# Late constants, filler products and another place for one maximum in a three-stage kernel of attention, mixture of experts and MLP

## The chip, the cores and the metric

The kernel runs on one core of a Trainium2 chip. The time is that of one execution on the device, in microseconds (us). Its engines are TensorE (PE), VectorE (DVE), ScalarE (ACT), GpSimd (POOL) and SyncE (SP, which here only issues transfers). Each runs its own instructions in the order in which they are written, and waits for the others by semaphores.

## The reference

Three stages in a row: an attention over 32 memory slots, a mixture of 8 experts of which each token takes its two best, and a dense MLP.

```python
# attention: q, k, v (4, 8, 576, 64), phi (4, 8, 576, 32)
a = exp(phi - max(phi, axis=seq));  a /= sum(a, axis=seq) + 1e-9
k_m = einsum('bhsm,bhsd->bhmd', a, k);  v_m = einsum('bhsm,bhsd->bhmd', a, v)
attn = softmax(q @ k_m.T / 8);  x = (attn @ v_m)  as (2304, 512)
# experts: w1 (8, 512, 1024), w2 (8, 1024, 512)
logits = x @ w_gate + log1p(exp(x @ w_noise)) * noise
top2, weights = the two largest of 8, softmax over the two
x = sum over the two of weight * (relu(x @ w1[e]) @ w2[e])
# MLP: w_in (512, 2048), w_out (2048, 512)
h = x @ w_in;  out = (h * clip(h + 3, 0, 6) / 6) @ w_out
```

## The kernel before

Attention runs in 8 groups, each one batch and 4 of its heads. A group has the stages a1 (phi transposed and its exponential, L541), q (q transposed on PE, L557), a2 (the weights e transposed on DVE, L579, then the product km of k and v with them on PE, 144 small matmuls, L585, and kd from it, L589), b (scores and softmax, with POOL's multiplications at L634 and L643) and c (output, written to DRAM as xf, L650 to L677). A routing (L686) follows two batches each: logits, the two largest, and each token's place in its expert's list, by one-hot products on PE (L737 to L799) with the constants tri, io12 and tok12. It ends in lists of token numbers, ids0 for the first two tiles of expert 0 after the first two batches, and ids for all.

An expert takes up to 608 tokens, 5 tiles. Its rows are gathered by an indirect DMA that POOL issues (L840), transposed on PE (L857) for experts 0 and 1 and by DMA for the others. Layer 1 (L874) and layer 2 (L924) split each 32-bit value into two 16-bit ones; for layer 1 each PSUM result is evacuated twice by ACT (L881 hf, L882 hh) and once by DVE (L884). Two tiles of expert 0 run early, beside the second routing. A weight matrix (w1 or w2 of an expert) comes in four pieces of 1 MB; its absolute maximum gives a power-of-two scale (`scale_w`, L424), and ACT (L418) and DVE (L420) write its two halves. The maximum over partitions goes either over PE (a diagonal of the 128 maxima, wdg, times ones, L434, and a reduction on DVE) or over POOL (an all-reduce, L438).

The order of work is made ahead of time by a list scheduler in the kernel's own code (`Sched`, L92). Operations are listed in program order with estimated durations and dependences; `sch.op(engine, duration, function, reads, writes)` lists one. The number `rush` of an operation shifts its due time, and `ORDER` (L37) says at which step which stage of which group is listed. What is not listed, as all constants here (L306 to L350), stands ahead of everything else on its engine. Among the constants are 34 warm-up products of 128 columns on PE (L303), DVE's ident, identh, identb, tri, p6, tok and ioc, POOL's casts io12 and tok12, and an all-reduce `first` whose result isn't used.

Of the kernel before, what the change touches and what calls it, by code (L numbers as in the profile page):

```python
# [35 lines left out]
CG = 2.0 ** -25  # L36
ORDER = (('ld', -1), ('b', 1), ('r', 6), ('q', 0), ('a1', -1), ('c', 3), ('a2', 0))  # L37
W0 = (4, 9)
# [5 lines left out]
WARM = 34  # L44
RUSH = {'w0': -15.0, 'w1': -346.0, 'r0': 121.0, 'r1': 173.0, 'x0': 103.0, 'e1': -46.0, 'e2': 203.0, 'a': (-50.0, -60.0, -45.0, -20.0, -30.0, -25.0, 40.0, -30.0)}
W0G = (4, 7)
CDMA = 1
EAT = (9, 12, 13)

# [216 lines left out]
def dve(n, mode=1):  # L266
    return 0.15 + n / 960.0 / mode
# [15 lines left out]
def attn_moe_kernel(ctx, tc, q, k, v, phi, w_gate, w_noise, noise, w1, w2, w_in, w_out, out):  # L283
# [16 lines left out]
    with tc.tile_pool(name="warm", bufs=1, space=bass.MemoryType.PSUM) as wp:  # L300
        pw = wp.tile([128, 128], F32, name="pw")
        for i in range(WARM):
            PE.matmul(pw, onesh, onesh, start=True, stop=True)  # L303

# [13 lines left out]
    identh = const.tile([128, 128], F16, name="identh")  # L318
    DVE.tensor_copy(identh, ident)
    identb = const.tile([128, 128], BF16, name="identb")  # L320
    DVE.tensor_copy(identb, ident)
    onesb = const.tile([128, 128], BF16, name="onesb")
# [10 lines left out]
    tri = const.tile([PT, PT], F16, name="tri")  # L333
    DVE.tensor_scalar(tri, iof[:PT, :PT], iop[:PT, 0:1], None, op0=ALU.is_gt)
    tok = const.tile([PT, B * NJ], F32, name="tok")
    p6 = const.tile([PT, 1], F32, name="p6")
    DVE.tensor_scalar(p6, iop[:PT, 0:1], float(NJ), float(-NT // 2), op0=ALU.mult, op1=ALU.add)
    for b in range(B):
        DVE.tensor_scalar(tok[:, b * NJ:(b + 1) * NJ], iof[:PT, :NJ], p6, float(S * b), op0=ALU.add, op1=ALU.add)
    ef = iof[:PT, :NE]  # L340
    ioc = const.tile([PT, NE * NTI], F32, name="ioc")
    DVE.tensor_scalar(ioc, iof[:PT, :NE * NTI], float(BIG * NTI), None, op0=ALU.subtract)
    io12 = const.tile([PT, 128 + NE * NTI, 2 * NJ], F16, name="io12")
    POOL.tensor_copy(io12[:, :128], iof[:PT, :, None].to_broadcast([PT, 128, 2 * NJ]))
    POOL.tensor_copy(io12[:, 128:], ioc[:, :, None].to_broadcast([PT, NE * NTI, 2 * NJ]))
    tok12 = const.tile([PT, B // 2, 2 * NJ], F16, name="tok12")
    POOL.tensor_copy(tok12, tok.rearrange("p (b j) -> p b j", b=B // 2))

    first = const.tile([128, 1], F32, name="first")
    POOL.partition_all_reduce(first, c3, channels=128, reduce_op=RED.absmax)  # L350
    bsum = const.tile([PT, B // 2, NE], F16, name="bsum")
# [37 lines left out]
    def new(nm, shape, dtype=F32):  # L389
        return T[nm].new(shape, dtype)  # L390
# [33 lines left out]
    def scale_w(am, deps, inv=2.0 ** -13, pe=False):  # L424
# [4 lines left out]
        if sch.seg == 0 or pe:  # L429

            wd, px = new("wdg", [128, 128], BF16), new(PS[sch.seg][2], [128, 128])
            sch.op("DVE", 0.25, lambda: DVE.tensor_scalar(wd.t, identb, ar.t[:, 0], None, op0=ALU.mult), [(ar, 0)], [wd],
                   lat=2.0 if inv < 1.0 else 0.0)
            sch.op("PE", 0.06, lambda: PE.matmul(px.t, onesb, wd.t, start=True, stop=True), [wd], [px], lat=0.12)  # L434
            sch.op("DVE", dve(128), lambda: DVE.tensor_reduce(ar.t[:, 1], px.t, axis=AX.X, op=ALU.max), [px], [(ar, 1)])  # L435
            pow2_ops(lambda: sm.t, lambda: DVE.tensor_scalar(sm.t[:, 0], ar.t[:, 1], TINY, None, op0=ALU.max), sm, [(ar, 1)], inv)
            return sm
# [28 lines left out]
    def stage_w1(e, w=None, acts=()):  # L466
        return stage_w(w1[e].rearrange("(c p) f -> p c f", p=128), "st0", w, acts)

# [72 lines left out]
    def stage_a1(g, ld):  # L541
# [144 lines left out]
    def route(b):  # L686
# [48 lines left out]
        def f():  # L735
# [4 lines left out]
            for j in range(NR - 1):  # L740
                n = NR - 1 - j
                PE.matmul(pv[:, j + 1:], onesh[:PT, :PT], mh.t[:, j, None, :].to_broadcast([PT, n, NE]),
                          start=False, stop=(n == 1))
        sch.op("PE", 1.0, f, [mh] + sums[:b] + [padk] * b, [pc])

# [38 lines left out]
        for h in range(2):  # L784
            ohb = new("ohb", [PT, 128 + 2 * nn, n12], F16)
            pv = lambda k, h=h: pqh.t[:, k, h][:, None, :]
            dv(64 * n12, lambda ohb=ohb, pv=pv: DVE.tensor_tensor(
                ohb.t[:, :128], io12[:, :128], pv(0).to_broadcast([PT, 128, n12]), op=ALU.is_equal), [(pqh, 0)], [(ohb, 0)])
            dv(nn // 2 * n12, lambda ohb=ohb, pv=pv: DVE.tensor_tensor(
                ohb.t[:, 128:128 + nn], io12[:, 128:], pv(1).to_broadcast([PT, nn, n12]), op=ALU.is_equal),  # L790
                [(pqh, 1)], [(ohb, 1)])
            dv(nn // 2 * n12, lambda ohb=ohb: DVE.tensor_tensor(
                ohb.t[:, 128 + nn:], ohb.t[:, 128:128 + nn],
                tok12[:, b][:, None, :].to_broadcast([PT, nn, n12]), op=ALU.mult),
                [(ohb, 1)], [(ohb, 2)])

# [40 lines left out]
    def gather(e, t0, nt, xT, idx, ikey, xfdeps, rows=NT):  # L837
        for t in range(nt):
# [6 lines left out]
            if e >= TDMA:  # L845
# [480 lines left out]
```

## Time and profile before

| | us |
|---|---|
| median of 3 runs | 914.17 (913.0 to 914.32) |
| profiled execution | 912.39 |
| its span, first to last instruction | 910.2 |
| PE busy | 874.0 |
| DVE busy | 617.8 |
| ACT busy | 436.8 |
| POOL busy | 142.6 |

The trace is of the profiled execution. Where a row of the timeline has several instructions of one line in a row, they are one row with their count; its duration reaches from the start of the first to the end of the last. A bracket at a row's end says how long the engine idled ahead of it, and what released it. PEclk is the clock granted to PE, 1.00 for 2.4 GHz and 0.50 for 1.2 GHz.

### The profile page before, as it was taken

Reading aid. Unit: us, or ns where it says so; the run is one execution under the profiler, and the core shown is the slowest. Engines: PE = TensorE matmul, PEld = TensorE weight load, DVE = VectorE, ACT = ScalarE, POOL = GpSimd, SP = SyncE. Lnnn points to the kernel's source line nnn. Section 1 sums busy time; section 2 is a strip of 40 time slices with the busy share of each in tenths; the row PEclk is TensorE's granted clock in tenths of the full one; section 3 lists DMA queues with packets and bytes.
Section 4 is the critical chain, followed back from the end, with each engine's and each line's share of the span. In section 5 each row is a group of like instructions: output and inputs, shape, how many; then the busy total and the mean of one; then the engine's idle time right before and its main releaser. Section 6 shows DMA issues by size and latency. Waiting matters only on the chain. (4 is left out here: it accounts for less than half of the span.)

```text
span 910.2 us, 16317 instructions
## 1 busy us (share of the span) xinstructions
PE 874.0 (96%) x6612; PEld 516.3 (57%) x6612; DVE 617.8 (68%) x1088; ACT 436.8 (48%) x665; POOL 142.6 (16%) x156
## 2 busy tenths in 40 slices
PE   7899599989999999999999999999999999999997
PEld 6676375564746565565756555555555555555553
DVE  5798975959688868688798889886464543333332
ACT  2386426656756657383646555554332422322322
POOL 2234311312032211000001131442010000000000
PEclk8999799999999999999999999999999999999999
DMA  9955335858878676949567463462210300300101
GB/s 343 351 187 175 101 122 202 270 147 254 224 201 274 157 262 169 274 93 295 196 244 221 159 221 133 114 150 59 75 38 1 79 1 10 61 1 1 35 1 38
DMA packets 109537, 135.14 MB, mean 148 GB/s; under 512 B 53008, under 2 KB 74000, under 8 KB 109456
## 3 DMA queue, kind: packets, MB, share of 16 engines
q1 hardware_dynamic: 103200, 114.43, 40.9%
q0 software_dynamic: 6144, 19.40, 7.7%
q8 instruction: 54, 0.88, 0.4%
q14 instruction: 27, 0.22, 0.1%
q10 hardware_dynamic: 112, 0.20, 0.1%
HBM read 94.74 MB, written 27.86 MB: 135 GB/s over the span
## 5 line engine op out<-in xcount | busy, mean ns | idle before, releaser
L1015 PE MATMUL two<-xT,wa 128*128 128x384 f16 x1152 | 195.1, 326 | 0.0
L1041 PE MATMUL o<-wb,hh 128*128 128x512 f16 x864 | 194.1, 379 | 0.0
L1015 PEld LDWEIGHTS <-wa 128*128 128x128 f16 x1152 | 112.6, 98 | 79.5 <-DVE hh L1025 0.2
L1041 PEld LDWEIGHTS <-hh 128*128 128x128 f16 x864 | 84.1, 98 | 96.3
L924 PEld LDWEIGHTS <-hh 128*128 128x128 f16 x720 | 69.7, 98 | 80.2 <-issue 2.5
L1022 ACT ACTIVATE hf<-hf,c 128x768 f32<-128x768 f32 x48 | 44.9, 935 | 145.2 <-DVE hf L1020 135.0
L1020 DVE TENSOR_TENSOR hf<-two,ivb 128x768 f32<-128x768 f32 x48 | 45.9, 956 | 92.1 <-PE two L1015 92.1
L874 PE MATMUL two<-xT,wb 128*128 128x304 f16 (+2 forms) x768 | 103.8, 295 | 3.3 <-ACT hh L882 3.2
L874 PEld LDWEIGHTS <-wb 128*128 128x128 f16 x768 | 75.8, 99 | 31.5 <-issue 3.9
L874 PEld LDWEIGHTS <-wa 128*128 128x128 f16 x768 | 75.9, 99 | 29.7 <-DVE war L435 1.7
L874 PE MATMUL two<-xT,wa 128*128 128x304 f16 (+1 forms) x672 | 90.1, 295 | 0.5 <-DVE war L435 0.5
L924 PE MATMUL o<-wb,hh 128*128 128x512 f16 x384 | 86.3, 379 | 0.0
L884 DVE TENSOR_TENSOR hh<-hf,hh 128x608 f16<-128x608 f32 (+2 forms) x72 | 49.5, 689 | 45.6 <-ACT hh L882 38.2
L924 PE MATMUL o<-wa,hh 128*128 128x512 f16 x336 | 75.3, 379 | 0.0
L840 POOL DMA_INDIRECT xg<-xf,ids x40 | 51.5, 1288 | 142.9 <-DVE ya L849 71.7
L881 ACT ACTIVATE hf<-two 128x608 f32<-128x608 f32 (+2 forms) x72 | 42.9, 596 | 55.3 <-PE two L874 53.0
L1025 DVE SCALAR_TENSOR_TENSOR hh<-hf,two 128x768 f32<-128x768 f32 x48 | 45.7, 951 | 29.8 <-ACT hf L1022 29.7
L1028 DVE TENSOR_TENSOR hh<-hh,hh 128x768 f16<-128x768 f32 x48 | 45.9, 955 | 29.4 <-ACT hh L1027 29.4
L1027 ACT ACTIVATE hh<-hh 128x768 f16<-128x768 f32 x48 | 40.4, 842 | 40.3 <-DVE hh L1025 40.3
L420 DVE SCALAR_TENSOR_TENSOR wb<-st,wsm,wb 128x1024 f16<-128x1024 f32 x40 | 50.5, 1280 | 4.5 <-ACT wb L418 3.2
L420 DVE SCALAR_TENSOR_TENSOR wa<-st,wsm,wa 128x1024 f16<-128x1024 f32 x40 | 51.3, 1310 | 1.4 <-ACT wa L418 1.4
L418 ACT ACTIVATE wb<-st,wsm 128x1024 f16<-128x1024 f32 x40 | 44.6, 1143 | 8.8 <-DVE wsm L406 3.6
(221 smaller groups left out, 1075.8 us busy)
## 6 DMA issues: line engine op xcount, KB each, us to landing
st<-moe_w_d SPq DMA_DIRECT2D x32, 1024.0 KB
ys<-yt SPq DMA_DIRECT2D x32, 256.0 KB
w<-moe_w_in_d SPq DMA_DIRECT2D x16, 512.0 KB
wf<-w64o SPq DMA_DIRECT2D x32, 256.0 KB
w<-moe_w_out_d SPq DMA_DIRECT2D x16, 512.0 KB
st<-wf SPq DMA_DIRECT2D x8, 1024.0 KB
kv<-k_d SPq DMA_DIRECT2D x8, 576.0 KB
kv<-v_d SPq DMA_DIRECT2D x8, 576.0 KB
```

The lines of the kernel that those rows point to most:

```text
L418: sch.op("ACT", act(1024, ptr=1), lambda s=s, w=w, c=c: ACT.activation(w.t[:, 0, c], s.t[:, c], AF.Copy, scale=sm.t[:, 2]), [(s, i), (sm, ...
L420: sch.op("DVE", 1.28, lambda s=s, w=w, c=c: DVE.scalar_tensor_tensor(w.t[:, 1, c], s.t[:, c], sm.t[:, 2], w.t[:, 0, c], op0=ALU.mult, op1= ...
L840: sch.op("POOL", 1.05, lambda t=t, xg=xg, tw=tw: POOL.indirect_dma_start(out=xg.t[:tw], out_offset=None, in_=xf[:rows], in_offset=bass.Ind ...
L874: PE.matmul(ph.t[:, i, :nw], wa.t[:, wi, c * 1024 + fb * 128:c * 1024 + fb * 128 + 128], xT.t[:, 4 * xi + c, o0 + i * nw:o0 + (i + 1) * nw ...
L884: sch.op("DVE", dve(n), lambda: DVE.tensor_tensor(hh.t[:, 1], hf.t, hh.t[:, 0], op=ALU.subtract), [hf, (hh, 0)], [(hh, 1)])
L924: PE.matmul(py.t[:tw], hs[fb].t[:, hi, tsl], wb.t[:, wi, fb * 512:(fb + 1) * 512], start=(fb == 0 and n == 0), stop=(fb == 7 and n == 2))
L1015: PE.matmul(ph.t[:, i, :CW], win[fb // 8].t[:, wi, o:o + 128], xT.t[:, 4 * xi + kc, :CW], start=(n == 0), stop=(n == 11))
L1020: sch.op("DVE", dve(768), lambda: DVE.tensor_tensor(t1.t, ph.t[:, :, :CW], ivb.t[:, None, :CW].to_broadcast([128, 2, CW]), op=ALU.mult), [ ...
L1022: o = sch.op("ACT", act(768, ptr=1), lambda: ACT.activation(t1.t, t1.t, AF.Relu, bias=c3, scale=CG), [], [t1])
L1025: sch.op("DVE", dve(768), lambda: DVE.scalar_tensor_tensor(gf.t, t1.t, 6.0 * CG, ph.t[:, :, :CW], op0=ALU.min, op1=ALU.mult), [t1, ph], [gf])
L1028: sch.op("DVE", dve(768), lambda: DVE.tensor_tensor(g.t[:, 1], gf.t, g.t[:, 0], op=ALU.subtract), [gf, (g, 0)], [(g, 1)])
L1041: PE.matmul(po[m_].t, g.t[:, gi, i, m_ * 128:(m_ + 1) * 128], wou[fb // 8].t[:, wi, (fb % 8) * 512:(fb % 8 + 1) * 512], start=(fb == 0 and ...
```

## The change

The warm-up gets ten more products of 512 columns. Before the first early transposes PE gets three listed operations of five products of 512 columns each, of ones with ones, into the transposes' own PSUM tile; they depend on ids0. Six constants become listed operations, DVE's four behind the transposed weights e of group 0, POOL's two behind DVE's. `first` is dropped. The maximum of the third expert's w1 (`e == 2`) goes over PE instead of POOL. The tables that set the listing change as a whole; of them the routing's step in ORDER (6 to 5) and the early layer's in EAT (12 to 11) stand for the others.

```diff
-ORDER = (('ld', -1), ('b', 1), ('r', 6), ('q', 0), ('a1', -1), ('c', 3), ('a2', 0))
+ORDER = (('b', 1), ('q', 0), ('c', 3), ('a2', 0), ('ld', -1), ('a1', -1), ('r', 5))
 WARM = 34
+WARM2 = 10
+FILL = 3
-EAT = (9, 12, 13)
+EAT = (9, 11, 13)
...
-        pw = wp.tile([128, 128], F32, name="pw")
+        pw = wp.tile([128, 4, 128], F32, name="pw")
         for i in range(WARM):
-            PE.matmul(pw, onesh, onesh, start=True, stop=True)
+            PE.matmul(pw[:, 0], onesh, onesh, start=True, stop=True)
+        for i in range(WARM2):
+            PE.matmul(pw, onesh, onesh[:, None, :].to_broadcast([128, 4, 128]), start=True, stop=True)
...
-    first = const.tile([128, 1], F32, name="first")
-    POOL.partition_all_reduce(first, c3, channels=128, reduce_op=RED.absmax)
...
-        return stage_w(w1[e].rearrange("(c p) f -> p c f", p=128), "st0", w, acts)
+        return stage_w(w1[e].rearrange("(c p) f -> p c f", p=128), "st0", w, acts, e == 2)
...
+    def late_consts(after):
...
+        for eng, dur, fn, r, w in (
+                ("DVE", 0.45, idb, [], idbk),
+                ("DVE", 0.3, lambda: DVE.tensor_scalar(tri, iof[:PT, :PT], iop[:PT, 0:1], None, op0=ALU.is_gt), [], trik),
+                ("DVE", 0.22, lambda: DVE.tensor_scalar(ioc, iof[:PT, :NE * NTI], float(BIG * NTI), None, op0=ALU.subtract),
+                 [], iock),
+                ("DVE", 0.75, toks, [], tokk),
+                ("POOL", 2.2, io, [iock], io12k),
+                ("POOL", 0.2, lambda: POOL.tensor_copy(tok12, tok.rearrange("p (b j) -> p b j", b=B // 2)), [tokk], tok12k)):
+            o = sch.op(eng, dur, fn, r, [w])
+            if eng == "DVE":
+                o.after.add(after)
...
-        sch.op("DVE", dve(576), lambda: DVE.transpose(e.t.rearrange("p i m -> p (i m)"), aT.t), [aT], [e])
+        o = sch.op("DVE", dve(576), lambda: DVE.transpose(e.t.rearrange("p i m -> p (i m)"), aT.t), [aT], [e])
+        if g == 0:
+            late_consts(o)
...
             px = new(PS[sch.seg][2], [128, 4, 128])
+            if sch.seg == 0 and e == 0 and t0 + t == 0:
+
+                for _ in range(FILL):
+                    def f(px=px):
+                        for _ in range(5):
+                            PE.matmul(px.t, onesh, onesh[:, None, :].to_broadcast([128, 4, 128]), start=True, stop=True)
+                    sch.op("PE", 1.07, f, [ikey], [px])
```

How the order moves is seen at three places. On DVE at the start, first before, then with the change (st holds a group's sums, aT its exponentials, e their transpose; L545 is L536 after, L579 is L598, L553 is L544):

```order
L317 TENSOR_SCALAR ident<-iof,iop 128x128
L334 TENSOR_SCALAR tri<-iof,iop 96x96
L319 CAST identh<-ident 128x128
L321 CAST identb<-ident 128x128
L337 TENSOR_SCALAR p_151<-iop 96x1
L339 TENSOR_SCALAR tok<-iof,p_151 96x6 x4
L545 STREAM_TRANSPOSE aT_209<-ph_196 128x576
L546 TENSOR_REDUCE st_214<-aT_209 128x1
L579 STREAM_TRANSPOSE e_224<-aT_209 128x576
L552 TENSOR_SCALAR st_214<-st_214 128x1
L553 RECIPROCAL st_214<-st_214 128x1
```

```order
L321 TENSOR_SCALAR ident<-iof,iop 128x128
L536 STREAM_TRANSPOSE aT_205<-ph_192 128x576
L537 TENSOR_REDUCE st_210<-aT_205 128x1
L598 STREAM_TRANSPOSE e_220<-aT_205 128x576
L543 TENSOR_SCALAR st_210<-st_210 128x1
L544 RECIPROCAL st_210<-st_210 128x1
L558 CAST identb<-ident 128x128
L559 CAST identh<-ident 128x128
L566 TENSOR_SCALAR tri<-iof,iop 96x96
L567 TENSOR_SCALAR ioc<-iof 96x40
L536 STREAM_TRANSPOSE aT_304<-ph_197 128x576
```

The five constants that stood ahead of group 0's transpose now stand behind its reciprocal, around group 1's transpose; ioc comes later too.

On ACT in layer 1 of the second expert (L881 and L882 evacuate a result, L847 prepares gathered rows of the third expert, L418 is the first scaled copy of a piece of the third expert's w1, wa), before and after (there L909, L910, L868 and L409):

```order
L881 ACTIVATE hf_2593<-two_2521 128x608
L882 ACTIVATE hh_2595<-two_2521 128x608
L418 ACTIVATE wa_2597<-st_3_2362,wsm_2563 128x1024
L847 ACTIVATE ya_2600<-xg_2513 128x512
L881 ACTIVATE hf_2627<-two_2566 128x608
L882 ACTIVATE hh_2630<-two_2566 128x608
L418 ACTIVATE wa_2597<-st_3_2362,wsm_2563 128x1024
```

```order
L909 ACTIVATE hf_2760<-two_2700 128x608
L910 ACTIVATE hh_2765<-two_2700 128x608
L868 ACTIVATE ya_2768<-xg_2616 128x512
L909 ACTIVATE hf_2778<-two_2735 128x608
L910 ACTIVATE hh_2780<-two_2735 128x608
L496 ACTIVATE w64a_2794<-w_2_2621 128x512
L868 ACTIVATE ya_2874<-xg_2690 128x512
L409 ACTIVATE wa_2879<-st_3_2385,wsm_2872 128x1024 x4
```

The four copies of w1 stood between the evacuations and now stand behind the last of the layer.

On POOL at the first all-reduce of a weight's maximum (war; an ISA row without a tile is the configuration instruction ahead of it, L840 or L861 a gather), before and after:

```order
L840 DMA xg_2432<-xf,ids 128x512
L840 DMA xg_2513<-xf,ids 128x512
L840 DMA xg_2546<-xf,ids 96x512
L438 ISA
L438 ISA war_2550<-war_2550 128x1
L840 DMA xg_2558<-xf,ids 128x512
L840 DMA xg_2632<-xf,ids 128x512
```

```order
L861 DMA xg_2690<-xf,ids 128x512
L861 DMA xg_2762<-xf,ids 128x512
L861 DMA xg_2782<-xf,ids 128x512
L861 DMA xg_2882<-xf,ids 96x512
L429 ISA
L429 ISA war_2935<-war_2935 128x1
L429 ISA war_3069<-war_3069 128x1
```

The configuration and the first all-reduce move behind the five gathers of the next expert, and the all-reduce is now that of the third expert's w2.

## Rows read from the trace of the kernel before

**Rows 1.** The page, busy time of each engine.
```profile
PE 874.0 (96%) x6612; PEld 516.3 (57%) x6612; DVE 617.8 (68%) x1088; ACT 436.8 (48%) x665; POOL 142.6 (16%) x156
```

**Rows 2.** Windows: busy us of PE, PEld, DVE, ACT, POOL; PEclk, DMA share, GB/s.
```profile
8.00:9.00 1.00, 0.00 (x0) 0.00 (x0) 0.33 (x1) 0.63 (x2) 0.00 (x0) 0.70 1.01 406
9.00:15.00 6.00, 5.45 (x104) 5.49 (x108) 2.39 (x7) 0.87 (x2) 0.00 (x0) 0.50 1.06 359
46.00:91.00 45.00, 42.69 (x785) 31.78 (x783) 41.26 (x110) 34.68 (x65) 16.40 (x14) 1.00 0.54 179
104.00:117.00 13.00, 6.13 (x29) 4.07 (x28) 10.47 (x33) 6.21 (x9) 3.35 (x2) 0.50 0.23 58
193.00:196.00 3.00, 3.00 (x14) 1.77 (x13) 3.00 (x4) 3.00 (x5) 0.32 (x1) 0.50 0.72 175
229.00:400.00 171.00, 171.00 (x1250) 106.18 (x1248) 130.26 (x199) 104.85 (x158) 29.54 (x26) 1.00 0.72 208
```

**Rows 3.** Timeline of PE: start us, us, what, and idle time before.
```profile
0.99 3.81 PE L303 MATMUL pw<-onesh 128*128 128x128 f16 x34 [0.99 <-POOL onesh L299]
...
9.55 6.88 PE L585 MATMUL oa<-kv,e 32*32 32x128 f32 x144 [4.74 <-DVE st L552]
...
37.40 4.13 PE L585 MATMUL oa<-kv,e 32*32 32x128 f32 x144
```

**Rows 4.** Timeline of DVE and POOL at the start.
```profile
3.29 1.50 POOL L344 CAST io<-iof 96x1536 f16<-96x1536 f32 x1
3.30 1.56 DVE L334 TENSOR_SCALAR tri<-iof,iop 96x96 f16<-96x96 f32 x1
...
6.18 0.77 DVE L545 STREAM_TRANSPOSE aT<-ph 128x576 f32<-128x576 f32 x1
...
22.49 1.16 POOL L634 TENSOR_TENSOR sc<-sc,sm 128x576 f32<-128x576 f32 x1 [15.73 <-DVE sm L633]
```

**Rows 5.** DMA from 0 to 30 us: GB/s in 40 slices of 0.75 us.
```profile
GB/s 0 0 101 316 412 381 332 338 338 390 384 406 418 436 374 208 301 316 393 424 409 406 399 412 439 363 388 349 396 436 409 406 350 140 31 74 326 406 406 326
```

**Rows 6.** Timeline of PE, POOL and DVE at the first gather and early layer.
```profile
105.06 1.35 POOL L840 DMA_INDIRECT xg<-xf,ids  x1 [7.64 <-DMA xf<-hl]
...
108.79 1.09 PE L857 MATMUL oa<-ident,xg 128*128 128x128 f32 x4 [4.51 <-DMA xg<-xf,ids]
111.19 1.09 PE L857 MATMUL oa<-ident,xg 128*128 128x128 f32 x4 [1.31 <-DMA xg<-xf,ids]
...
113.69 5.89 PE L874 MATMUL da<-xT,wa 128*128 128x256 f16 x35 [0.36 <-DVE xT L861]
...
117.40 0.23 DVE L727 TENSOR_TENSOR mh<-mk 96x96 f16<-96x96 f32 x1
...
119.41 0.21 PE L737 MATMUL oa<-mh,tri 96*96 96x96 f16 x1
...
120.16 4.09 PE L874 MATMUL da<-xT,wa 128*128 128x256 f16 x36
...
132.50 5.34 PE L924 MATMUL oa<-wa,hhe 128*128 128x512 f16 x24
```

**Rows 7.** L438's instructions, then the timeline of POOL, PE and ACT around it.
```profile
L438 POOLq MODIFY_POOL_CONFIG  x2: 43/43/43, 182.3 to 182.3; - x2
...
182.78 6.62 PE L874 MATMUL two<-xT,wb 128*128 128x304 f16 x50
188.72 0.41 POOL L438 PARTITION_ALL_REDUCE war<-war  x1 [6.70 <-issue]
189.72 1.15 ACT L418 ACTIVATE wa<-st,wsm 128x1024 f16<-128x1024 f32 x1 [5.23 <-DVE wsm L406]
192.57 7.64 PE L874 MATMUL two<-xT,wb 128*128 128x304 f16 x45 [3.16 <-ACT hh L882]
203.53 2.75 PE L924 MATMUL o<-wb,hh 128*128 128x512 f16 x12
...
227.06 3.26 PE L874 MATMUL two<-xT,wa 128*128 128x304 f16 x24
```

More of the change, by code (lines that the diff above doesn't have):

```diff
@@ L44 @@
 WARM = 34
-RUSH = {'w0': -15.0, 'w1': -346.0, 'r0': 121.0, 'r1': 173.0, 'x0': 103.0, 'e1': -46.0, 'e2': 203.0, 'a': (-50.0, -60.0, -45.0, -20.0, -30.0, -25.0, 40.0, -30.0)}
+WARM2 = 10
+FILL = 3
+RUSH = {'w0': -22.0, 'w1': -195.0, 'r0': 256.0, 'r1': 623.0, 'x0': 357.0, 'e1': -60.0, 'e2': 195.0, 'a': (-35.0, -40.0, -45.0, -25.0, -20.0, -10.0, 110.0, -5.0)}
 W0G = (4, 7)
 CDMA = 1
-EAT = (9, 12, 13)
+EAT = (9, 11, 13)
 def _atanh_coefs(n=5):
@@ L318, in attn_moe_kernel @@
     identh = const.tile([128, 128], F16, name="identh")
-    DVE.tensor_copy(identh, ident)
     identb = const.tile([128, 128], BF16, name="identb")
-    DVE.tensor_copy(identb, ident)
     onesb = const.tile([128, 128], BF16, name="onesb")
@@ L333, in attn_moe_kernel @@
     tri = const.tile([PT, PT], F16, name="tri")
-    DVE.tensor_scalar(tri, iof[:PT, :PT], iop[:PT, 0:1], None, op0=ALU.is_gt)
     tok = const.tile([PT, B * NJ], F32, name="tok")
     p6 = const.tile([PT, 1], F32, name="p6")
-    DVE.tensor_scalar(p6, iop[:PT, 0:1], float(NJ), float(-NT // 2), op0=ALU.mult, op1=ALU.add)
-    for b in range(B):
-        DVE.tensor_scalar(tok[:, b * NJ:(b + 1) * NJ], iof[:PT, :NJ], p6, float(S * b), op0=ALU.add, op1=ALU.add)
     ef = iof[:PT, :NE]
     ioc = const.tile([PT, NE * NTI], F32, name="ioc")
-    DVE.tensor_scalar(ioc, iof[:PT, :NE * NTI], float(BIG * NTI), None, op0=ALU.subtract)
     io12 = const.tile([PT, 128 + NE * NTI, 2 * NJ], F16, name="io12")
-    POOL.tensor_copy(io12[:, :128], iof[:PT, :, None].to_broadcast([PT, 128, 2 * NJ]))
-    POOL.tensor_copy(io12[:, 128:], ioc[:, :, None].to_broadcast([PT, NE * NTI, 2 * NJ]))
     tok12 = const.tile([PT, B // 2, 2 * NJ], F16, name="tok12")
-    POOL.tensor_copy(tok12, tok.rearrange("p (b j) -> p b j", b=B // 2))
-    first = const.tile([128, 1], F32, name="first")
-    POOL.partition_all_reduce(first, c3, channels=128, reduce_op=RED.absmax)
     bsum = const.tile([PT, B // 2, NE], F16, name="bsum")
@@ L431, in scale_w @@
             wd, px = new("wdg", [128, 128], BF16), new(PS[sch.seg][2], [128, 128])
-            sch.op("DVE", 0.25, lambda: DVE.tensor_scalar(wd.t, identb, ar.t[:, 0], None, op0=ALU.mult), [(ar, 0)], [wd],
+            sch.op("DVE", 0.25, lambda: DVE.tensor_scalar(wd.t, identb, ar.t[:, 0], None, op0=ALU.mult), [(ar, 0), idbk], [wd],
                    lat=2.0 if inv < 1.0 else 0.0)
@@ L555, in stage_a1, with toks, idb, io @@
         return st, aT
+    idbk, trik, tokk, iock, io12k, tok12k = [sch.keep() for _ in range(6)]
+    def late_consts(after):
+        def toks():
+            DVE.tensor_scalar(p6, iop[:PT, 0:1], float(NJ), float(-NT // 2), op0=ALU.mult, op1=ALU.add)
+            for b in range(B):
+                DVE.tensor_scalar(tok[:, b * NJ:(b + 1) * NJ], iof[:PT, :NJ], p6, float(S * b), op0=ALU.add, op1=ALU.add)
+        def idb():
+            DVE.tensor_copy(identb, ident)
+            DVE.tensor_copy(identh, ident)
+        def io():
+            POOL.tensor_copy(io12[:, :128], iof[:PT, :, None].to_broadcast([PT, 128, 2 * NJ]))
+            POOL.tensor_copy(io12[:, 128:], ioc[:, :, None].to_broadcast([PT, NE * NTI, 2 * NJ]))
+        for eng, dur, fn, r, w in (
[9 more added lines that the diff above has]
+                o.after.add(after)
     def stage_q(g, ld):
@@ L743, in f @@
                           start=False, stop=(n == 1))
-        sch.op("PE", 1.0, f, [mh] + sums[:b] + [padk] * b, [pc])
+        sch.op("PE", 1.0, f, [mh, trik] + sums[:b] + [padk] * b, [pc])
         def count(terms, keys, fn, w):
@@ L787, in route @@
             dv(64 * n12, lambda ohb=ohb, pv=pv: DVE.tensor_tensor(
-                ohb.t[:, :128], io12[:, :128], pv(0).to_broadcast([PT, 128, n12]), op=ALU.is_equal), [(pqh, 0)], [(ohb, 0)])
+                ohb.t[:, :128], io12[:, :128], pv(0).to_broadcast([PT, 128, n12]), op=ALU.is_equal), [(pqh, 0), io12k], [(ohb, 0)])
             dv(nn // 2 * n12, lambda ohb=ohb, pv=pv: DVE.tensor_tensor(
                 ohb.t[:, 128:128 + nn], io12[:, 128:], pv(1).to_broadcast([PT, nn, n12]), op=ALU.is_equal),
-                [(pqh, 1)], [(ohb, 1)])
+                [(pqh, 1), io12k], [(ohb, 1)])
             dv(nn // 2 * n12, lambda ohb=ohb: DVE.tensor_tensor(
@@ L794, in route @@
                 tok12[:, b][:, None, :].to_broadcast([PT, nn, n12]), op=ALU.mult),
-                [(ohb, 1)], [(ohb, 2)])
+                [(ohb, 1), tok12k], [(ohb, 2)])
             def f(ohb=ohb, h=h):
```

## The prediction

> **What bounds the kernel now.** I read the page first: TensorE (PE) is busy for 874.0 of 910.2 us [rows 1], so what a change of order can win lies in the 36 us in which PE stands, and in the stretches in which it runs at half its clock. The table of windows says where these are: from 229 us on PE has no gap (171.00 of 171.00 us in 229 to 400), while the granted clock is 0.50, the lower of its two levels (1.2 instead of 2.4 GHz), in 9 to 15, 104 to 117 and 193 to 196 us [rows 2]. Each of these three follows a standstill of PE, and the timeline of each place says what PE waited for.
>
> At the start, 34 warm products end at 4.80 (0.99 + 3.81). PE then idles 4.74 us to 9.55, when the first km product (L585) has its operand. The product takes 6.88 us; the same 144 matmuls take 4.13 later [rows 3]. At the first gather, PE waits 4.51 and 1.31 us for gathered rows, and the first 35 products of the early layer run at 5.89 us where 36 later take 4.09 [rows 6]. At the third expert's first weight, PE waits 3.16 us and runs slowly after it [rows 7]. Between the first two, from 46 to 91 us, VectorE (DVE) and PE share the limit, busy 41.26 and 42.69 of the 45 us [rows 2]; work that enters this stretch earlier leaves it earlier if neither gets more to do.
>
> **The start.** Before, DVE runs tri, identh, identb, p6 and tok ahead of group 0's first transpose (L545), which starts at 6.18; from there to the product at 9.55 is a chain of 3.37 us [rows 3, 4]. The change puts these constants behind group 0's transposed weights. DVE is then free at about 3.3, where tri starts, and the chain alone would give a product at 6.7. It also needs phi, k and v of group 0, together 1.47 MB (288, 576 and 576 KB). The transfer rates of 0.75 us each sum to 1.41 MB by 6.0 us and 2.15 MB by 8.0 [rows 5]. Served strictly in order the operands are there at 6.2; if the transfers share the engines with the ones issued behind them (phi of group 1, then q, 2.36 MB with these) v comes later. I take 8.0, between 6.7 and the 9.55 of before, since what lies ahead of v and half of what follows is through by then: gain 1.5 us, bounds 0 and 2.85.
>
> The warm block grows by ten products of 512 columns. At 24 in 5.34 us [rows 6] they take 2.2 us, so PE works to 7.0 and idles some 1.0 us instead of 4.74. Before, the clock held for the first 3.2 us of idling: it is mixed, 0.70, only in the slice 8 to 9 [rows 2]. I expect it to hold, and km to take 4.13 instead of 6.88: gain 2.75, bounds 0 and 2.75. Sum of the start: 4.25 us.
>
> Is this handed on? The constants (2.9 us of DVE before, from 3.30 to 6.18, standing beside POOL among it) fall where DVE waits: it ran 2.39 us in the six from 9 to 15 [rows 2]. The transfers up to v of group 1 are 3.5 MB, which the rates reach before 12 us [rows 5], ahead of a second product at 15.3 (19.6 less 4.25). So the cover holds; if it fails, all 4.25 are lost, which is the first rival.
>
> Two prices hang on the move. First, GpSimd's (POOL's) casts into io12 now run beside group 1's DVE work. In the trace tri, 96x96, took 1.56 us beside the first cast of 1.50 [rows 4], though DVE's operations of this size on the routing take 0.23, as mh [rows 6]. POOL's casts are this one, 1,536 columns, and one of 480, some 2.0 us at that rate. So up to 2.0 us of DVE can be blocked near 8 to 10.5 us, and group 1's next need is at km's end, 12.1; DVE would then be late by 0 to 0.7 us. I take 0. The Trainium skill, SBUF — State Buffer, "SBUF: two separate sides", says why this can recur: VectorE in some modes and GpSimd share a port pair as an exclusive lock, and whoever comes second stands for the whole instruction. The trace's 1.56 beside 1.50 agrees, and by the rule the sum would be 0.7 us smaller. Second, the configuration instruction ahead of POOL's first tensor_tensor has its cost hidden somewhere in the 15.73 us that POOL waits for DVE until 22.49 [rows 4]. It now stands behind the casts, at about 10.6. At the 6.4 us that the other configuration of the trace took (182.3 to 188.72, [rows 7]) it is over at 17.0, before the need at 18.2 (22.49 less 4.25), 7.6 after 10.6. Cost 0, with an upper end of 15.7 - 7.6 = 8.1 us.
>
> **Routing, fillers and the first gather.** The first gather starts at 105.06; its last releaser by the trace is the write of xf, not ids0 [rows 6]. Listing route(0) a step sooner moves about six of its DVE operations, of mh's 0.23 us each, ahead of attention work, some 1.4 us, but if xf's write binds, the gather comes no sooner. I take 0, bounds 0 and -1.4 us. The fillers are 15 products of 512 columns behind ids0 and ahead of the first transposes: 3.3 us at full clock, 6.7 at half. They need ids0 alone, which the gather needs too, so they start no later than it, and the rows arrive 3.7 us after 105.06 (at 108.79): at full clock nothing is delayed. At half clock the first transposes come 3.0 us late, but the second, at 111.19, wait for their own rows; the end slips by 0.5 at most. What they buy is the clock. 35 products at full clock take 35/36 of 4.09 = 3.98, so 1.91 us is won there, and half of the second transposes' 1.09, together 2.4. Next in the way is the routing of the last batches: its mh ended at 117.63 and its product L737 ran at 119.41 [rows 6], so 1.8 us of slack is met by products 2.4 us earlier, and up to 0.6 is given back, since mh's chain itself waits for evacuations of these products only in part. Gain 1.8, bounds +0.5 (a loss) and -3.8 us with the earlier list.
>
> **The third expert.** Before, w1's maximum is an all-reduce on POOL, which idles 6.70 us after its configuration at 182.3 and starts at 188.72. DVE's L440 stands for it, and the first scaled copy on ScalarE (ACT, L418) behind that for 5.23 us to 189.72. Behind this copy in ACT's order are the evacuations of expert 1's layer 1, so PE stops for 3.16 us [rows 7]. Then 45 products take 7.64 us; at the 6.62/50 of those before it is 5.96, so the clock costs 1.68. The change takes this maximum with a PE product of 128 columns (0.2 us) in layer 2, and its four ACT copies stand behind all eight pairs of evacuations. Gain 3.16 + 1.68 = 4.84 us, bounds 3.2 and 4.84: the clock's part depends on the standstill alone.
>
> The configuration isn't saved, it moves to w2 of the third expert. There it stands behind 20 gathers, in layer 2 of expert 1, by the order some 6 us after that layer's start. At 6.4 us it ends at about 12.8, the scale is out at 15 to 16, and four copies of 1.15 us on ACT end at 20. Behind them in ACT's order are outputs of later tiles and then expert 2's first evacuation, which was due 23.5 us after layer 2's start (203.53 to 227.06, [rows 7]). So some 3 us of cover are left, and I count 0. The Trainium skill, GPSIMD Engine Reference, "2.1 Instruction dispatch", says that the first call into freshly loaded GpSimd code pays about 6 us of loading that no instruction shows. The trace agrees (6.4 us to the start, 6.70 idle). By that rule each change of POOL's code pays again wherever it stands, and with the cover gone the third expert's gain would be 0.
>
> **Sum.** 4.25 + 1.8 + 4.84 = 10.9 us. The profiled run took 912.39 (its span 910.2 and 2.2 around it), the median is 914.17, so the one gives 901.5 and the other 903.3. I predict at the median: **903.3 us**. Least gains: 0 + 0 (with -0.5) + 3.2, less 0.7, is 2.0; most: 5.6 + 3.8 + 4.84 = 14.2.
>
> **Rivals.**
> - The start's gain is lost, all or in part (chance 0.20). The warm block ends before v arrives by more than I think, and the clock falls anyway: 906.1. Or group 1 waits for its own transfers and all 4.25 goes: 907.6. For it: the DMA engines are full from 2 to 24 us. Against: the sums of [rows 5].
> - POOL's configuration takes back in layer 2 what it gave in layer 1 (0.10). If the loading starts 3 us later than I read it, ACT's copies reach expert 2's evacuations; at 6 to 7 us later PE stops again for 3.2 and runs slow for 1.7: 908.1. For it: the cover is the thinnest of all. Against: the gathers ahead of it are listed for an expert two steps on.
> - Slower than before (0.07): POOL's configuration ahead of group 0's first tensor_tensor really takes the 15.7 us that the trace leaves room for. Then attention stands 8.1 us at the start, the clock falls again, the half-clock prices come back (2.75 for a km product and 1.7 for what follows), and POOL's casts add their 0.7: 914.2 - 10.9 + 8.1 + 4.5 + 0.7 = 916.6, with no change ending at 916.0. It decides from a load of some 15 us; under 7.6 it costs nothing. The single load that the trace shows took 6.4.
> - The change doesn't do what it says (0.07): the numbers of the planner also move weight preparation of the later experts. PE has no gap there today, so they can only cost; 9 to 11 us of new waits would end at 912 to 914, of which 0.05 is within the bound.
>
> **How the numbers follow.** The forecast has 0.56. The lower end is 900.0: 903.3 less 1.4 for the sooner gather and 1.3 for the start's bound, and 0.6 for mh, is 900.0. The upper end is 909.0, which takes in the first two rivals with the 0.7 of the casts. About 0.18 is left out. A difference of 0.2%, 1.8 us, is about what can be told from no change. Faster than 912.3: 0.56 + 0.20 + 0.10 + 0.02 = 0.88; same 0.05; slower 0.07.
>
> **What will show it.** Right: the first km product starts near 8 us and takes 4.1; the granted clock is 1.00 in 9 to 15; the first early products run at 0.114 us each; no wait of PE for ACT in expert 1's layer 1, and the all-reduce's 6.7 us standing in layer 2 with PE at work. Wrong: a km product of over 6 us, a DVE or POOL wait of several us at 17 to 25 us, a first gather that isn't 4 us sooner than 105.06, or new PE waits beyond 229 us.

## The result and the profile after

The changed kernel takes 904.02 us at the median (902.5 to 905.97), the kernel before in the same comparison 913.95; the ratio is 0.9905 with a 95% interval from 0.9888 to 0.9921. Forecast was 903.3 us, a gain of 10.9; measured is 9.9. Two later comparisons gave 0.9897 (0.9873 to 0.9922) and 0.9898 (0.9880 to 0.9916), gains of 8.5 and 8.9 us. The sum came out nearly right. Its terms did not: each of the three was forecast too large.

The profiled execution of the changed kernel took 905.97 us with a span of 904.2. The page of after, busy time of each engine (before: [rows 1]):

```profile
span 904.2 us, 16357 instructions
PE 878.0 (97%) x6638; PEld 516.9 (57%) x6638; DVE 617.7 (68%) x1090; ACT 436.4 (48%) x665; POOL 144.5 (16%) x154
```

PE idles 26 us instead of 36. Its timeline at the start (before: [rows 3]):

```profile
0.99 3.81 PE L305 MATMUL pw<-onesh 128*128 128x128 f16 x34 [0.99 <-POOL onesh L301]
4.59 2.92 PE L307 MATMUL pw<-onesh 128*128 128x512 f16 x10
8.17 4.13 PE L606 MATMUL oa<-kv,e 32*32 32x128 f32 x144 [0.66 <-DMA kv<-v_d]
...
15.44 3.89 PE L606 MATMUL oa<-kv,e 32*32 32x128 f32 x130
21.20 0.63 PE L606 MATMUL oa<-kv,e 32*32 32x128 f32 x14 [1.87 <-issue]
...
26.34 5.74 PE L606 MATMUL oa<-kv,e 32*32 32x128 f32 x144
```

The first km product starts at 8.17 and takes 4.13 us, as forecast. But the third takes 5.74: the half clock has come back, later. The windows of after in five stretches (columns as in [rows 2]; the clock is the third number from the end) show where:

```profile
6.00:15.00 9.00, 7.44 (x179) 5.75 (x176) 5.28 (x20) 2.39 (x6) 0.78 (x2) 1.00 1.04 360
20.00:30.00 10.00, 7.10 (x122) 5.42 (x126) 6.86 (x22) 3.65 (x8) 2.31 (x2) 0.83 1.03 393
87.00:97.00 10.00, 6.96 (x37) 4.62 (x36) 9.51 (x42) 3.66 (x8) 5.00 (x7) 0.83 0.44 123
100.00:118.00 18.00, 13.53 (x91) 8.92 (x92) 15.27 (x49) 8.10 (x17) 4.54 (x5) 0.81 0.47 154
190.00:198.00 8.00, 7.40 (x56) 5.28 (x54) 6.98 (x10) 4.95 (x10) 2.81 (x2) 1.00 1.10 315
```

To see where the time went I cut the span of two profiles of before (this one and run r5) and three of after (this one, r1 and r9) at the starts of the same PE instructions: the first routing's second group of one-hot products, the second routing's product with tri (L737 before, L758 after), expert 0's layer 1 on its late tiles, expert 2's layer 1. Us from one to the next, gains by the means:

| stretch | before | after | gain | forecast |
|---|---|---|---|---|
| start to one-hot products | 103.18, 102.89 | 101.48, 100.68, 99.61 | 2.45 | 4.25 |
| to second routing's product | 16.23, 16.02 | 15.53, 15.26, 15.61 | 0.66 | 1.8 |
| to expert 0's layer 1 | 23.02, 23.00 | 23.00, 23.00, 23.00 | 0.0 | 0 |
| to expert 2's layer 1 | 84.63, 84.23 | 80.80, 80.54, 80.49 | 3.82 | 4.84 |
| to the end | 683.14, 684.06 | 683.39, 683.32, 683.49 | 0.2 | 0 |

That is 7.1 us; the medians say 8.5 to 9.9, 9.1 in the mean. The profiled executions of after lie 0 to 2 us above the medians of their runs (905.97 to 904.02, 904.55 to 904.55, 904.02 to 902.95), 1.0 in the mean; those of before lie 0.6 below theirs in the mean (912.39 to 913.95, 912.29 to 911.95); and the time outside the span is 0.4 us shorter after (1.8 instead of 2.1 to 2.2). Together these are the difference. What the new listing of the tables contributes to each stretch was not tried apart from the named changes.

### The profile page after: what moved, and what is told of

It is laid out like the page before. It is cut to its first block, busy times and chain, and to the rows that moved or that the text cites. A ratio compares the mean times of both kernels' runs of the same rounds, so it can differ in the third digit from the quotient of the medians.

```text
span 904.2 us, 16357 instructions
## 1 busy us (share of the span) xinstructions
PE 878.0 (97%) x6638; PEld 516.9 (57%) x6638; DVE 617.7 (68%) x1090; ACT 436.4 (48%) x665; POOL 144.5 (16%) x154
## 5 line engine op out<-in xcount | busy, mean ns | idle before, releaser
L861 POOL DMA_INDIRECT xg<-xf,ids x40 | 55.5, 1387 | 126.7 <-DVE ya L870 44.3
L909 ACT ACTIVATE hf<-two 128x608 f32<-128x608 f32 (+2 forms) x72 | 42.9, 596 | 63.2 <-PE two L902 60.3
L409 ACT ACTIVATE wa<-st,wsm 128x1024 f16<-128x1024 f32 x40 | 44.0, 1142 | 7.7 <-DVE wsm L397 7.7
```

The lines of the kernel that those rows point to most:

```text
L409: sch.op("ACT", act(1024, ptr=1), lambda s=s, w=w, c=c: ACT.activation(w.t[:, 0, c], s.t[:, c], AF.Copy, scale=sm.t[:, 2]), [(s, i), (sm, ...
L861: sch.op("POOL", 1.05, lambda t=t, xg=xg, tw=tw: POOL.indirect_dma_start(out=xg.t[:tw], out_offset=None, in_=xf[:rows], in_offset=bass.Ind ...
```

## The experiments

In all variants of the changed kernel every instruction but those named stands where it stood.

**Both kernels again (r1, r9, r5).** Unchanged sources, for more profiles.

> The changed kernel once more, for a second profile. In the first profile its execution took 905.97 us, the slowest of four (902.5 to 905.97), and PE ran at half its clock in four stretches (26 to 30, 91 to 95, 101 to 105, 111 to 116 us). Theory A: where the clock falls differs between executions of the same kernel, and this makes the spread: 902 to 906 again, with the half-clock stretches at other places or fewer of them in a faster profile. Theory B: the stretches belong to the kernel: the same four places within 0.5 us, and the spread has another cause.

> The changed kernel a third time, beside the two with more fillers on one chip: 902.5 to 905, and again one half-clock stretch in 21 to 30 us, one in 87 to 95 and one or two in 101 to 116.

> The kernel before once more, for a second profile. Its first profile came from an execution of 912.39 us, below the median of its runs (913 to 914). Theory A: the stretches at half clock differ between executions, so a second profile has another set (for example one after the wait for vb at 89 to 92 us, which the first did not have) and a time in 911 to 916. Theory B: they belong to the kernel, and the same three stretches stand there (9 to 15, 104 to 117, 193 to 196 us).

Measured: 904.55 and 902.95 us for the changed kernel. The stretches at half clock stand in the same parts of the program but not at the same places of it: in 20 to 30 us the mean clock was 0.83, 0.66 and 0.66 in the three profiles, in 100 to 118 it was 0.81, 0.91 and 0.81. Before, again, 911.95 us; windows of this run:

```profile
6.00:15.00 9.00, 5.45 (x112) 5.48 (x116) 4.43 (x12) 1.73 (x4) 0.43 (x4) 0.62 1.04 381
20.00:30.00 10.00, 7.42 (x192) 5.87 (x188) 6.85 (x19) 3.19 (x7) 2.34 (x2) 1.00 0.81 307
87.00:97.00 10.00, 7.11 (x37) 4.66 (x35) 9.96 (x39) 4.04 (x8) 4.79 (x7) 0.83 0.43 120
```

It has a stretch after the wait for vb (clock 0.83 in 87 to 97) that the first profile of before did not have. (vb is the operand of the output products of stage c, and POOL writes it.) So theory A holds: after a given standstill the clock falls in one execution and not in another, for 1.5 to 3.5 us of PE's time each. Not all of this arrives: behind that wait twelve products take 4.54 us in r5 and 2.99 in the first profile, yet from their start to the second one-hot products it is 11.12 and 11.10 us, because at full clock PE waits for DVE twice on the way. One profile of each kernel does not tell differences of this size.

**Without the ten wide warm-up products (r3), and before with them (r7).**

```diff
-WARM2 = 10
+WARM2 = 0
```

> The changed kernel with the 34 small warm-up products alone, the ten wide ones left out, every other instruction in its place. PE would end its warm-up at 4.8 and idle to 8.2. Theory A: the clock falls, the first km product takes 5 to 6.9 us instead of 4.13, and of these 0.9 to 2.75 us some is hidden again, because POOL's configuration (10.6 to 21.1 us in the first profile) holds group 0's scores anyway: 0 to 1.5 us slower than the changed kernel. Rival B: the whole 2.75 us arrive at the end: 906.7.

> The kernel before with the ten wide warm-up products alone, every other instruction in its place. PE works to 7.0 and idles to 9.5. Theory A (the clock holds through the first km product, but the same half clock comes later, after the next standstill of PE, as in the run without the ten products): the km product takes 4.13 instead of 6.88, the second one starts 2.7 us sooner, and of these 0 to 1.5 us are left at the first gather. Rival B (as predicted): all 2.75 us arrive at the first gather (102.3 instead of 105.06) and at the end.

Measured: r3 904.94 us (ratio 0.9898 to before, as the changed kernel's 0.9897 beside it); r7 912.15, ratio to before 1.0002 (0.9987 to 1.0017). PE's timeline of r3 at the start:

```profile
7.05 6.81 PE L606 MATMUL oa<-kv,e 32*32 32x128 f32 x144 [2.25 <-DVE st L543]
...
16.99 4.12 PE L606 MATMUL oa<-kv,e 32*32 32x128 f32 x140
23.27 0.41 PE L606 MATMUL oa<-kv,e 32*32 32x128 f32 x4 [2.16 <-issue]
...
27.03 3.15 PE L606 MATMUL oa<-kv,e 32*32 32x128 f32 x108
```

The last row is the first 108 of the third km product's 144, as far as this view reached. The same 108 in r1:

```profile
26.00 4.19 PE L606 MATMUL oa<-kv,e 32*32 32x128 f32 x108
```

And of r7:

```profile
9.54 4.13 PE L587 MATMUL oa<-kv,e 32*32 32x128 f32 x144 [2.00 <-issue]
...
22.86 1.06 PE L587 MATMUL oa<-kv,e 32*32 32x128 f32 x14 [2.16 <-issue]
23.86 2.18 PE L570 MATMUL da<-ident,qt 128*128 128x128 f32 x9
```

The ten products do what they should: 4.13 us instead of 6.5 to 6.9. But where the first product is fast, a stretch at half clock follows the standstill in the second one (1.9 to 2.4 us; "issue" says that the engine waited for nothing that the profile shows). Three later profiles (r6, r10, r11 below) are the exception. It does not always take the same instructions: in r7 the nine transposes of q (2.18 us instead of 1.20), in the changed kernel's three profiles the transposes (1.20, 1.84, 1.68) and the third km product (5.74, 5.17, 5.60). Where the first is slow, as in r3, all of this runs at full clock. In the first profile of the changed kernel another 1.14 us of the lead goes in a wait of PE for kd, which DVE writes late. In r3 the first c product starts at 40.89, in r1 at 40.91: the 2.7 us are given back within 34 us. Rival B of both runs falls; r7 decides it, with an interval of 1.4 us to either side, where r3 and r1 have some 2 us each. What r7's profile kept at the one-hot products (101.68 against 102.89 and 103.18) and at the first gather (103.57 against 104.77 and 105.06) theory A had allowed; it does not show in its median.

**POOL's configuration earlier (r4).** One tiny operation on POOL ahead of its casts.

```diff
+    early = const.tile([128, 1], F32, name="early")
+    POOL.tensor_tensor(early, c3, c3, op=ALU.mult)
```

> The changed kernel with one tiny tensor_tensor on POOL ahead of its casts, so that the configuration is loaded from 3.2 us on and not from 10.6; every other instruction in its place. Theory A (the loading takes some 10 us and held group 0's scores, then DVE, then PE at 22 to 26 us): POOL's first scores product at 17.0 instead of 21.1, no wait of 4.6 us of DVE for ACT, the third km product at 24 to 25.5 instead of 26.3, and 1 to 3 us faster, 901 to 903. Rival B (from 46 us on DVE and PE set the pace, whatever arrives sooner waits there): within 0.5 us of the changed kernel, with the same time of the first gather (103.4).

Measured: 903.12 us (902.04 to 904.84), ratio 0.9877 (0.9853 to 0.9901), not to be told from r1's 0.9897. In the changed kernel (timeline of POOL and DVE, and the instructions of L655) the load is longer than I had taken it, and DVE stands for it:

```profile
L655 POOLq MODIFY_POOL_CONFIG  x2: 8/8/8, 10.6 to 10.6; - x2
...
21.14 1.15 POOL L655 TENSOR_TENSOR sc<-sc,sm 128x576 f32<-128x576 f32 x1 [10.57 <-issue]
...
23.04 0.75 DVE L658 TENSOR_REDUCE sm<-sc 128x18 f32<-128x576 f32 x1 [4.61 <-ACT sc L657]
```

In r4 POOL stands from 3.3 to 15.4 ahead of the added operation, and no longer ahead of the scores:

```profile
15.42 0.18 POOL L352 TENSOR_TENSOR early<-c 128x1 f32<-128x1 f32 x1 [12.15 <-issue]
...
17.66 1.15 POOL L657 TENSOR_TENSOR sc<-sc,sm 128x576 f32<-128x576 f32 x1
19.56 0.75 DVE L660 TENSOR_REDUCE sm<-sc 128x18 f32<-128x576 f32 x1 [1.23 <-ACT sc L659]
```

DVE's wait shrinks by 3.4 us, yet the one-hot products start at 100.80, amid the 99.61 to 101.48 of the changed kernel. So the wait was real and, alone, cost nothing that arrives: rival B of this run stands. The comparison is not clean, since the clock in 20 to 30 us was 0.66 in r4 and 0.83 in the first profile of the changed kernel; r10 and r11 below, both at 1.00 there, repeat it with the same outcome.

**Without the fillers (r2), and with more of them (r6, r10, r11).** r2 leaves the 15 products out. r6 and r10 (the same kernel) add 13 ahead of the c products that wait for vb, 8 between the early transposes and 3 and 3 around the early layer's first product; r11 has r4's operation too.

```diff
+GAP = (8, 3, 3, 13)
...
+                for _ in range(GAP[3] if g == 6 and i == 0 else 0):
+                    PE.matmul(po.t[:, 0].rearrange("p (a b) -> p a b", a=4), onesh[:, :PT],
+                              onesh[:, None, :].to_broadcast([128, 4, 128]), start=True, stop=True)
...
+            n1 = GAP[0] if sch.seg == 0 and e == 0 and t0 + t == 1 else 0
...
+                for _ in range(n1):
+                    PE.matmul(px.t, onesh, onesh[:, None, :].to_broadcast([128, 4, 128]), start=True, stop=True)
...
+        gaps = GAP[1:] if sch.seg == 0 and fb == 0 else (0, 0)
...
+                    for _ in range(gaps[m_] if m_ < 2 else 0):
+                        PE.matmul(ph.t[:, 1].rearrange("p (a b) -> p a b", a=4), onesh,
+                                  onesh[:, None, :].to_broadcast([128, 4, 128]), start=True, stop=True)
```

> The changed kernel without the 15 filler products, every other instruction in its place. As predicted (fillers hold the clock and win 1.8 us): 905.5 to 906. Theory A (after the first profile: the clock falls all the same around the early layer, since PE idles again between the two transposes and before the first product): within 0.7 us of the changed kernel, 903.5 to 904.7. Rival B (the fillers delay the transposes): 0.3 us or more faster, the first transposes sooner than 3.7 us after the first gather's start.

> The changed kernel with more fillers, every other instruction in its place: 13 products of 512 columns ahead of the c products that wait for vb (87.5 to 90.6 us), 8 between the two early transposes, 3 ahead of the early layer's first product and 3 behind it. Theory A (PE idles there and the clock then falls, in three of the profiles by 1.7 to 3.4 us of time): no half clock in 88 to 95 and 110 to 116; from the second one-hot product to the second batch's routing product 13.0 to 13.7 us instead of 15.3 to 15.5; 2 to 4 us faster, 900.5 to 902.5. Rival B (products of ones do not hold the clock, or delay what they stand ahead of): the clock falls at the same places, and the time is the changed kernel's or 1 to 3 us longer.

> The kernel with more fillers again (13 products ahead of the c products that wait for vb, 8 between the early transposes, 3 and 3 around the early layer's first product). Theory A (each standstill of PE that is filled keeps the clock): 1.5 to 3.5 us under the changed kernel beside it, and from the second one-hot product to the second batch's routing product 13.9 us again. Rival B (its first result was a good draw of the stretches that vary): within 1 us of the changed kernel.

> More fillers and the early configuration of POOL together. Theory A (the configuration's 10 us cost something at 17 to 26 us): DVE's wait for ACT there 1.2 instead of 4.6 us, and 0.3 to 1 us under the kernel with more fillers. Rival B (what arrives sooner waits at 46 us or at vb): the same time within 0.5 us.

Measured: r2 904.18 us (902.41 to 908.52), ratio 0.9896, no difference to r1. r6 900.79 (ratio 0.9882, 0.9856 to 0.9909). On one chip r9 902.95, r10 901.34 (ratio 0.9886, 0.9869 to 0.9904), r11 899.28. By these intervals r6 and r10 alone are not told from the changed kernel (r9 0.9898, 0.9880 to 0.9916). The timeline of the changed kernel at the early layer (before: [rows 6]):

```profile
102.41 4.57 PE L880 MATMUL oa<-onesh 128*128 128x512 f16 x15
107.10 0.66 PE L885 MATMUL oa<-ident,xg 128*128 128x128 f32 x4
109.49 0.63 PE L885 MATMUL oa<-ident,xg 128*128 128x128 f32 x4 [1.74 <-DMA xg<-xf,ids]
110.80 0.27 PE L902 MATMUL da<-xT,wa 128*128 128x256 f16 x1 [0.68 <-ACT xT L887]
111.53 5.65 PE L902 MATMUL da<-xT,wa 128*128 128x256 f16 x35 [0.46 <-DVE xT L889]
```

Here the fillers hold the clock for the transposes (0.66 and 0.63 us instead of 1.09) and lose it behind them: PE idles 1.74, 0.68 and 0.46 us, and the 35 products take 5.65 us, hardly less than 5.89. In r2 they take 6.00 and the transposes 1.09, and the stretch from the one-hot products to the second routing's is 16.41 us against 15.26 to 15.61: the 15 fillers are worth 0.8 to 1.15 us there, which r2's median does not show. The waits alone do not make the clock fall. In r8 (below), whose order is the changed kernel's up to 190 us, PE idles 1.70, 0.69 and 0.46 us at the same places, and yet:

```profile
109.75 3.98 PE L904 MATMUL da<-xT,wa 128*128 128x256 f16 x35 [0.46 <-DVE xT L891]
```

There the stretch is 13.84 us. So with the 15 fillers alone the clock fell here in five profiles (this one, r1, r9, r3, r4) and held in one. In r6:

```profile
103.71 1.89 PE L891 MATMUL oa<-onesh 128*128 128x512 f16 x8
105.44 0.60 PE L893 MATMUL oa<-ident,xg 128*128 128x128 f32 x4
...
107.47 3.98 PE L914 MATMUL da<-xT,wa 128*128 128x256 f16 x35
```

With the gaps filled the 35 products take 3.98 us in all three profiles, to the hundredth what the prediction had put down for them, and the stretch is 13.90, 13.88 and 13.89 us in r6, r10 and r11, 1.4 to 1.7 under the changed kernel: theory A of r6 and r10 holds for this place. The clock in 87 to 97 us is 1.00 in all three, where it was 0.83 in all three of the changed kernel (but 1.00 in r2 too, without the 13 products). Beside the three profiles of the changed kernel these 13 are worth little: from the last c products ahead of the wait for vb to the second one-hot products it takes 14.80 to 14.82 us instead of 14.93 to 15.10 (but 15.82 in r4 and 16.19 in r3).

In these three the stretch at half clock in 20 to 30 us is missing too, 60 us ahead of the first added product. The third km product of r10:

```profile
25.13 4.13 PE L607 MATMUL oa<-kv,e 32*32 32x128 f32 x144
```

I see no way from the one to the other. It is worth more than the fillers: at the last c products ahead of the first added one the three stand at 82.60, 82.68 and 83.36 us, the changed kernel's three at 84.52 to 86.38, so 1.2 to 3.8 us of the lead in the profiles come before any added filler. The three differ from the rest already in the warm-up, where the ten wide products take 3.28 to 3.50 us, and 2.32 to 2.95 in the other profiles that have them; why the clock then holds, no run shows.

r11 has the lowest median of all (898.8 to 900.71; ratio 0.9859, 0.9841 to 0.9876, against the changed kernel's 0.9880 to 0.9916 beside it). It beats both kernels. That the early configuration adds the 2 us between r10 and r11, more than either theory allowed, is not shown: r11's one-hot products start at 98.16, r10's at 97.50. The medians differ with the mean granted clock of the executions: it was 0.996 in all four of r11 (898.8 to 900.71) and in one of r10's four, which took 899.87; the others of r10 had 0.991 to 0.992 and took 901.26 to 902.27. Whether the early configuration makes such executions more frequent is open.

**The third expert's maximum on POOL, in place (r8).** The all-reduce stands where PE's product stood; ACT's copies stay behind the evacuations.

```diff
-            sch.op("PE", 0.06, lambda: PE.matmul(px.t, onesb, wd.t, start=True, stop=True), [wd], [px], lat=0.12)
+            sch.op("PE", 0.06, (lambda: POOL.partition_all_reduce(ar.t[:, 1], ar.t[:, 0], channels=128, reduce_op=RED.absmax))
+                   if pool else lambda: PE.matmul(px.t, onesb, wd.t, start=True, stop=True), [wd], [px], lat=0.12)
```

> The changed kernel, but the maximum of the third expert's w1 taken by POOL's all-reduce again, at the place in the order where PE's product stood (after the first products of expert 1's layer 2); ACT's four copies stay behind all evacuations. POOL's configuration then stands in front of it. Theory A (what won the time is that the copies no longer stand between the evacuations, so a late scale holds nothing): the all-reduce comes 6.4 us after its configuration, ACT's copies some 6 us later than in the changed kernel, PE doesn't wait in layer 1, and the time stays within 0.7 us. Rival B (the engine that takes the maximum is what matters): a new standstill of PE of 3 us or more in layer 2 or at expert 2's start, 3 to 5 us slower, 907 to 909.

Measured: 909.86 us (907.36 to 913.42), ratio 0.9980 (0.9962 to 0.9997), so most of the change's gain is gone. Its timeline of POOL, ACT and PE in layer 2 of expert 1:

```profile
201.79 0.41 POOL L426 PARTITION_ALL_REDUCE war<-war  x1 [7.14 <-issue]
202.80 4.27 ACT L409 ACTIVATE wa<-st,wsm 128x1024 f16<-128x1024 f32 x4 [6.89 <-DVE wsm L397]
...
210.09 0.67 ACT L957 ACTIVATE yt<-o,iys 128x512 f32<-128x512 f32 x1
...
210.81 13.27 PE L954 MATMUL o<-wb,hh 128*128 128x512 f16 x48 [4.10 <-ACT yt L957]
```

ACT waits 6.89 us for the scale, then copies, and the output of layer 2 that stands behind the copies in its order comes so late that PE, which waits for that result to be read, stops 4.10 us. After that the clock is at half until some 216 us (0.50 in 211 to 216). From expert 0's to expert 2's layer 1 it takes 87.34 us (136.57 to 223.91) instead of 80.5 to 80.8. Rival B holds: the place behind the evacuations would not have been enough, the short way over PE is needed. Whether the short way alone, with the copies at their old place, would have been enough was not tried. The same rows of the changed kernel:

```profile
L429 POOLq MODIFY_POOL_CONFIG  x2: 32/32/32, 202.5 to 202.5; - x2
...
189.21 0.63 ACT L868 ACTIVATE ya<-xg 128x512 f16<-128x512 f32 x1 [3.64 <-DMA xg<-xf,ids]
...
191.03 6.36 PE L902 MATMUL two<-xT,wb 128*128 128x304 f16 x48 [0.60 <-ACT hh L910]
...
208.94 0.64 POOL L429 PARTITION_ALL_REDUCE war<-war  x1 [6.72 <-DVE w64o L505]
```

The configuration, now that of w2, is issued at 202.5, and its all-reduce starts at 208.94, 11.7 us after the layer's start at 197.22 (forecast 12.8). Its own operand was ready on DVE only at 208.0, so this trace does not show how long the load took. PE does not wait for it, and ACT waits 0.84 us for the scale that follows.

## Why the prediction was right, and where it was not

**The start.** Its steps came as forecast: the product at 8.17 (7.00 and 7.04 in the other two profiles, where v came sooner and the chain on DVE bound), 4.13 us for it, the second at 15.44, 14.26 and 14.30 against 15.3. The step that failed is "is this handed on?". I looked for late transfers and for DVE, and took the clock's 2.75 us as won. In the changed kernel's three profiles they are not: with the first product fast, the clock falls after a later standstill of PE, and the time is paid in the transposes of q and the third km product (r1, r9; r7 shows it on the kernel before). Where the clock did not fall in 20 to 30 us (r6, r10, r11), the one-hot products start 4.9 to 5.6 us sooner than before, so there the 4.25 did arrive. The first rival was right in its place but had the wrong cause. Of 4.25 us 2.45 arrived in the three, and these are the earlier start, not the clock: r3, which starts early without the clock's gain, has its one-hot products at 100.85, 2.2 us sooner than before. Two of the prediction's own signs of being wrong came: the first gather starts at 103.38, 102.56 and 101.51, which is 1.7 to 3.6 us sooner than 105.06 and not 4, and DVE waits several us near 20.

**Two prices of the move.** The casts cost nothing: the large one ran from 3.21 on, ahead of DVE's constants, and tri took 0.26 us. The rule from the Trainium skill, SBUF — State Buffer, "SBUF: two separate sides", that DVE in some modes and GpSimd block each other, cost nothing here: DVE's transpose and reduction beside the large cast took 0.78 and 0.75 us, as they do elsewhere. The configuration took 10.57 us (10.0 and 10.8 in r9 and r1), not 6.4, so it ended 4.2 us after the need at 16.95 (sm's end). This is the mechanism of the rival that ended slower, at half its length; it held DVE for 4.61 us, and r4, with r10 and r11, shows that this cost nothing by 100 us.

**Routing and fillers.** Forecast 1.8, measured 0.66. The mechanism was right, the size not: the fillers were to hold the clock until the products, and they stand only ahead of the first transposes. PE's later waits (1.74 and 0.68 us) I had in front of me in [rows 6] as 1.31 and counted as harmless; in r8 waits of that length were, in five other profiles not. With those filled the term is 2.1 to 2.3 us in all three profiles (13.9 against 16.02 and 16.23). The 0.6 us that I took off for the second routing was not given back: the stretch behind it is 23.00 to 23.02 us in both kernels.

**The third expert.** Forecast 4.84, measured 3.82. PE's standstill of 3.16 us shrank to 0.60 (0.35 and 0.30 in the others) and did not vanish: ACT now waits at L868 for a gathered tile, with evacuations behind it. What was next in ACT's order I had not asked. The clock stays at 1.00 in 190 to 198. Some 0.4 to 0.6 us of the difference is not placed (in r5 the standstill of before was 2.76 us, not 3.16).

**The reason that I gave** for this gain, the place of the copies, is only a part of it: r8 shows that the late scale would have held PE in layer 2 as well. The second rival's mechanism is thus real; it did not strike because w2's copies stand behind two of the layer's outputs in ACT's order, where w1's in r8 stood ahead of all.

**The total** came out at 904.0 against 903.3, with the gains by the medians 1.0 to 2.4 us smaller than forecast and those of the profiles 3.8 smaller. That the median fits so well is luck: each of the three terms was too large, and of three comparisons this one gave the largest gain, with single executions of the changed kernel from 902.2 to 907.2.

## What to carry to other kernels

A stretch at half clock that is taken away may come back after the next standstill: count its price as won only when several profiles show that the clock holds through the standstills that follow. Here it came back 14 to 18 us after the first product's start. If products of ones shall keep the clock, put them into each gap up to the work that they are meant for; here, written into that work's own result tile, they delayed nothing, and the clock held in three profiles of three instead of one of six. When a late value is moved off one place of an in-order queue, read what stands behind it at the new place.

## What the runs showed of the hardware

- Which standstill lets the clock fall varies between executions of one kernel: after the 2.9 us wait for vb it fell in one of two profiles of before, and after the waits of 1.7, 0.7 and 0.5 us at the early layer it held in one of six with the 15 fillers.
- POOL's configuration took 6.4 us at 182 us (6.0 in r5) and 6.9 at 195 (r8), and 10.6 and 12.2 us when it ran within the first 21 us, with the DMA engines full. The Trainium skill, GPSIMD Engine Reference, "2.1 Instruction dispatch", gives about 6 us for the first call into freshly loaded code. The loads at 182 and 195 us agree; at the start the measurement decides otherwise. That the transfers stretch it was not tried.
- In r3 the first km product took 6.81 us, as at half clock, while the clock in the windows of that stretch reads 1.00:

```profile
6.00:15.00 9.00, 7.95 (x155) 7.76 (x155) 4.58 (x17) 1.41 (x5) 0.78 (x2) 1.00 1.05 386
```

The clock's rows can miss a stretch; the duration of a known group of products is the safer reading. The warm-up is another case. In 1 to 5 us of the kernel before the clock's row reads 1.00, while the 34 products of 128 columns take 3.81 us [rows 3], 0.112 each; at the rate of the 24 products of 512 columns in [rows 6] it would be 0.056, half of that. The prediction's reading that the clock held while PE idled up to 8 us rests on the same rows.
